# Three edits to the attention stage of a fused attention and two-MoE kernel: the decay array, one GpSimd wait, and when x is loaded

## The chip, the core and the metric

The program runs on one core of one Trainium2 chip. Its time is the device time in microseconds of one launch, from all inputs in HBM to the output in HBM. The program was run three times before the change; a profiled execution of its own gives the trace.

## What is computed

The reference does three things one after the other: causal attention with a decay per token (4 batches of 8 heads, 576 tokens, head width 64), a gated feed-forward block on the result, and a second MoE block with eight experts that each take a fixed number of tokens.

```python
# attention: one of 32 heads (4 batches x 8 heads), S = 576, D = 64
scores = scale * np.matmul(q, k.transpose(0, 1, 3, 2))
cum = np.cumsum(np.log(np.clip(f, 0.0001, 1.0)), axis=-1)
scores = np.where(causal, -1e9, scores + cum[..., :, None] - cum[..., None, :])
attn = softmax(scores)                     # with the row maximum taken off
x = (attn @ v)                             # to 2304 tokens x 512
x = (sigmoid(x @ w_gate) * (x @ w_val)) @ w_out        # 512 -> 1536 -> 512
# second block: each token goes to one of 8 experts, 288 tokens each
out[mask_e] = np.maximum(x[mask_e] @ w1[e], 0) @ w2[e]
```

All matrix products are made in float32 precision from two rounded parts (`fp32r`): a high part that ScalarE rounds, and a low part that GpSimd gets by a subtraction.

## The kernel before

**Stages.** Attention takes the first 201 us. `network` (L1183) builds the stages in that order; instructions go to each engine in the order in which the code is written, so what stands where in the loop decides what waits behind what.

**Attention, one head.** `prep(h)` (L131, L132, L135) has ScalarE round the raw q and k of a head into the tile `P` (five of them rotate). `decay(h)` (L139) and `copies(h)` (L143, L145) are DMAs from SBUF to SBUF: the decay rows into `P`, and q and k into the tile `p`. `query_low(h)` (L148) and `key_low(h)` (L152) are GpSimd subtractions that put the low parts into `p`. `maxparts(h)` multiplies q and k for the row maxima, which VectorE reduces (L177, tiles `mj` and `mx`); for head 0 alone the decay is added by a second set of products of `pick` and `ck`, while later heads have it in `P`. `rows(h)` turns the maxima over with one product (`pb<-identr,mx`), ScalarE copies them out (L215, tile `mr`), and a DMA stores them as row 66 of `P` (L218, `P<-mr`). `scores(h)` multiplies (`py`, `p1b`), ScalarE takes the exponent (L240, tile `e`), GpSimd masks the diagonal blocks (L244), and `av(h)` multiplies with v (`pv<-e,vf`).

**Order of the loop.** In round h the code writes `scores(h)`, then `av(h-1)`. Inside the products of `av` stand `early()`, which has `rows(h+2)`, `prep(h+4)`, `decay(h+5)` and `fill(h, 1)`, and `late()`, which has the maxima of head h+3. Then come `copies(h+3)`, the store of finished outputs or loads of q, k and v, `query_low(h+4)`, `key_low(h+2)`, and last `fill(h, 0)`. So a head's maxima are stored in round h-2 and read at the start of round h. SyncE (SP) issues all these DMAs in that same order, one after the other.

**The decay.** `ft` takes the 32 rows of f twice, on 64 partitions (L74): the source is an access pattern with a first dimension of two and a stride of zero. VectorE clips it (L119), ScalarE takes the logarithm (L120), VectorE sums it up (L122) and writes the rounded decay `ck` (L123) and, on the lower 32 rows, what the rounding lost (L124). Nine products without a use (`warm`, `py<-identb`) run on TensorE meanwhile, and more stand between the first maxima.

**What `fill` does.** Between heads it prepares the next stage: it cuts weights of the gated block into high and low parts (45 steps on VectorE at L437, L440 and L443 for 15 pieces, each followed by L451 on ScalarE and L454 on GpSimd; the list `BITS` says how many steps come after which head), and it loads the x of batch 0. That x comes in four pieces of two heads: `X.load` (L484, L485) issues four DMAs of 128 KB for each (two of the attention output `xs` into `xal`, two of the reciprocal row sums `rec`, broadcast to 64 partitions); `X.split` multiplies them on VectorE (L498), rounds on ScalarE (L500) and subtracts on GpSimd (L502). Before, the four loads stand at the ends of rounds 23, 24, 25 and 26, and the multiplications in rounds 27 to 30.

Of the kernel before, what the change touches and what calls it, by code (L numbers as in the profile page):

```python
# [6 lines left out]
F32 = mybir.dt.float32  # L7
# [10 lines left out]
B, H, S, D = 4, 8, 576, 64  # L18
NHEAD = B * H
# [41 lines left out]
def attention(ev, qk, vr, f, xs, rec, fill, W):  # L61
# [3 lines left out]
    nc, tc = ev.nc, ev.tc  # L65
    with ExitStack() as ctx:
# [4 lines left out]

        W.third = st
        ft = st.tile([128, S], F32, name="ft")[:2 * NHEAD]
        nc.sync.dma_start(ft, bass.AP(tensor=f.tensor, offset=f.offset, ap=[[0, 2], [S, NHEAD], [1, S]]))  # L74

        RAW, VF = {}, {}
        RAW4 = [st.tile([128, 2, S], F32, name=f"raw{i}") for i in range(4)]
# [20 lines left out]
        idle = st.tile([2 * NHEAD, 1], F32, name="warm")  # L98
# [18 lines left out]
        ck = st.tile([2 * NHEAD, S], F32R, name="ck")  # L117
# [11 lines left out]
        def prep(h, key=False):  # L129
            p1, r = P1[h % 5], RAW[h]  # L130
            nc.scalar.activation(p1[0:64, Q0:K0], r[0:64], AF.Copy)  # L131
            nc.scalar.activation(p1[0:64, K0:], r[64:128], AF.Copy)  # L132
            P2[h] = wk.tile([128, 2 * S], F32R, name="p2", bufs=4)
            if key:
                nc.scalar.activation(P2[h][64:128, S:], r[64:128], AF.Copy)  # L135
# [5 lines left out]
        def copies(h, keys=True):  # L141
            p1, p2 = P1[h % 5], P2[h]
            nc.sync.dma_start(p2[0:64, :S].bitcast(F32), p1[0:64, Q0:K0].bitcast(F32))  # L143
            if keys:
                nc.sync.dma_start(p2[64:128, S:].bitcast(F32), p1[0:64, K0:].bitcast(F32))  # L145

        def query_low(h):
            nc.gpsimd.tensor_tensor(P2[h][64:128, :S], RAW[h][0:64], P1[h % 5][0:64, Q0:K0], op=OP.subtract)  # L148
# [147 lines left out]
        warm(WARM[0])  # L296
        prep(0, True)
        copies(0, False)
        query_low(0)
        prep(1, True)  # L300
        key_low(0)
# [86 lines left out]
TC = 512  # L388
# [786 lines left out]

EARLY = 15
KO = (0, 1, 3, 4, 2)
XL = 23
FIRST = {3: (0, 1), 6: (2,)}
BITS = [0] * 5 + [(3 * i + 1) // 2 for i in range(23)] + [34, 35, 38, 41, 45]  # L1180
PRE = 0


def network(tc, qk, vv, f, ww, bcT, w1, w2, cb, cf, out):
    nc = tc.nc
    ev = Env()
    ev.nc, ev.tc = nc, tc
    with ExitStack() as ctx:
        ctx.enter_context(tc.manual_schedule())

        def pool(name, stack=ctx, side="left", bufs=1, **kw):
            return stack.enter_context(tc.tile_pool(name=name, bufs=bufs, side=side, reuse_waits="tile", **kw))

        ev.consts = pool("consts")
        dr = ctx.enter_context(tc.tile_pool(name="dram", bufs=1, space=bass.MemoryType.DRAM))
        xs = dr.tile([NHEAD, D + 1, S], F32, name="xs")
        rec = dr.tile([NHEAD, S], F32, name="rec")
        x2d = dr.tile([N, DM], F32, name="x2d")
        L = ev.consts.tile([128, E, NT], F32, name="L")
        ev.idx = ev.consts.tile([TT, 24], I32, name="idx")  # L1200
        ev.consts.tile([128, 48], F32, name="space")

        body, right = ExitStack(), ExitStack()
        xp = pool("xp", right, "right")
        w0, mix = pool("w0", body), pool("mix", body)
        W = Weights(ev, mix, ww)
        W.tiles(w0, 0, -(-EARLY // 3))
        X = XLoader(ev, xp, xs, rec)
        xa = X.tiles(xp, "xa")
        X.put(0, xa)  # L1210
        X.put(2, xa)
        X.put(4, xa)

        xr = [None]

        def fill(h, lag):
            if lag == 0 and h in FIRST:
                for n in FIRST[h]:
                    W.load(n)
            if lag == 0:  # L1220
                if 0 <= h - XL - 4 < 4:
                    X.split(0, h - XL - 4, steps=(0,))
                for i in range(BITS[h], BITS[h + 1]):
                    W.bits(*divmod(i, 3))
                if 0 <= h - XL < 4:
                    if (h - XL) % 2 == 0:
                        xr[0] = W.third.tile([128, 2, S], F32, name=f"raw{(h - XL) // 2}")
                    X.load(0, h - XL, r=xr[0][:, (h - XL) % 2, :TC])
            else:
                if 0 <= h - XL - 5 < 4:  # L1230
                    X.split(0, h - XL - 5, steps=(1, 2))
                for lag, step in ((1, 0), (2, 1)):
                    if lag <= h < NHEAD + lag:
                        for i in range(BITS[h - lag], BITS[h - lag + 1]):
                            n, s = divmod(i, 3)
                            if s == 2:
                                W.cut(n, (step,))

        attention(ev, qk, vv, f, xs, rec, fill, W)
        W.third = None  # L1240

        W.tiles(pool("w1", body), -(-EARLY // 3), NF)
        work, ps = ExitStack(), ExitStack()
        xq = pool("xq", right, "right")
        W.more, W.ahead = xq, 4
        xb = X.tiles(xq, "xb")
        X.put(1, xb)
        X.put(3, xb)
        F = Ffn(ev, W, X, EARLY, bcT, x2d, L, pool("pg", ps, bufs=4, space=PSUM), pool("po", ps, space=PSUM))
        F.wk, F.mix, F.right = pool("fw", work), mix, xq  # L1250
        F.wp = F.wk.tile([128, 128], F32, name="wp")[:, :NF * E].rearrange("p (f e) -> p f e", e=E)
        F.regular()
        rest, left = F.defer(lambda: xd), 7 * 3 * NF

        def filler(n):
            nonlocal left
            for _ in range(min(n, left)):
                next(rest, 0)
                left -= 1

        F.group(filler)
        right.close()
        work.close()

        ep = pool("ep", side="right")
        tail = ExitStack()
        rp, rw = pool("rp", tail), pool("rw", tail, bufs=2)
        scratch = [mix.tile([128, n], F32, name=m, bufs=1) for m, n in (("mr0", 1024), ("mr1", 1024), ("mb0", 512), ("mb1", 512))]
        xd, scratch[0] = scratch[0][:, :DM], scratch[0][:, DM:]
        EW = Experts(ev, ep, w1, w2)  # L1270
        nc.vector.memset(xd, 0.0)
        F.store(LAST, xd)
        R = Route(ev, rp, rw, F.bank, cb, cf, scratch, filler)
        EW.load(0)
        F.logits(scratch[1], filler)
        R.start(L)
        for r in range(ROUNDS):
            R.round(r == 0, FILL[5] if r < ROUNDS - 1 else 6, lambda: r and EW.split((r - 1) // 2, (r - 1) % 2, R.c[:1, 0, :1, 0]))
        a = R.settle()
        R.permutation(a)  # L1280
        X0 = First(ev, ep, scratch, x2d)
        X0.tokens(R)
        for part in range(2):
            EW.split(3, part, X0.hot[:1, :1])
        filler(left - 2 * 3 * NF)
        X0.gather()
        filler(left)
        next(rest, 0)
        X0.turn(xd, F.bank)
        tail.close()  # L1290
        body.close()
        ps.close()
        EW.pool = pool("ew")
        xw = pool("xw", bufs=2)
        pools = {n: pool("xp_" + n, bufs=b, space=PSUM) for n, b in (("t", 3), ("y", 2), ("h", 3))}
        experts(ev, EW, x2d, X0.x, ev.idx, out, xw, lambda n: pools[n].tile([128, 512], F32, name="e" + n))


def layout(inputs):

    import numpy as np
    q, k, v = (np.asarray(inputs[n]).reshape(NHEAD, S, D) for n in "qkv")
    qk = np.concatenate([q.transpose(0, 2, 1), k.transpose(0, 2, 1)], 1).reshape(NPAIR, 2, 2 * D, S).transpose(0, 2, 1, 3)
    rows = np.r_[0:512, 448:576].reshape(5, 128)
    vv = v.reshape(NPAIR, 2, S, D)[:, :, rows].transpose(0, 3, 2, 1, 4)
    vv = np.concatenate([vv, np.ones(vv.shape[:-1] + (2,), vv.dtype)], -1)
    vv[:, :64, 4] = 0.0
    cols = [np.asarray(inputs[n]).reshape(4, 128, NF, 128).transpose(2, 1, 0, 3).reshape(NF, 128, 512)
            for n in ("moe_w_gate", "moe_w_val")]
    ww = np.concatenate(cols + [np.asarray(inputs["moe_w_out"]).reshape(NF, 128, DM)], 2)  # L1310
    cb, cf = route_constants()
    named = dict(qk=qk, vv=vv, f=np.asarray(inputs["f"]).reshape(NHEAD, S), ww=np.ascontiguousarray(ww).view(np.int64),
                 wg2=np.asarray(inputs["moe2_w_gate"]).T, w1=inputs["moe2_w1"], w2=inputs["moe2_w2"], cb=cb, cf=cf)
    return {n: np.ascontiguousarray(a) for n, a in named.items()}

# [12 lines left out]
```

## Time and profile before

| | |
|---|---|
| time, median of 3 runs | 906.77 us (906.17 to 911.58) |
| the profiled execution | 907.6 us, of which its span 905.9 us |
| TensorE busy | 879.4 us (97%) |
| VectorE, GpSimd, ScalarE busy | 59%, 50%, 38% |
| mean granted TensorE clock | 0.992 of full speed |
| moved by DMA | 110.99 MB, mean 123 GB/s |

TensorE is busy for 97% of the span, so its waits and its clock are read first. A busy TensorE is not one at its peak, since matmuls are pipelined and their ends modelled. Line numbers in the rows are those of the kernel before. `SPq` rows are DMA issues by SyncE: the time in them is that of the issue, not that of the transfer.

### The profile page before, as it was taken

To read this page: it belongs to the slowest core of one execution; us is meant where nothing else is said; L and a number is where in the kernel's file an instruction comes from. 1 tells how busy PE (TensorE), PEld (TensorE's weight loads), DVE (VectorE), ACT (ScalarE), POOL (GpSimd) and SP (SyncE) were. 2 spreads that over 40 slices of the span, in tenths; PEclk is the share of its full clock that TensorE was granted. 3 is DMA by queue.
4 is the path that set the end of the run, shared out by engine and by line. 5 is a ranking of instruction groups with operands and counts; after the bars stand their busy time and mean duration, and the time that the engine had idled before them with its cause. 6 is when DMAs were issued, how large, how long until landed. Compare 5 with 4: busy or idle time off the path is not lost. (4 is left out here: it accounts for less than half of the span.)

```text
span 905.9 us, 14131 instructions
## 1 busy us (share of the span) xinstructions
PE 879.4 (97%) x5193; PEld 748.7 (83%) x5193; DVE 535.7 (59%) x1182; ACT 343.8 (38%) x609; POOL 456.7 (50%) x387
## 2 busy tenths in 40 slices
PE   6999999889999999999999999999999999999995
PEld 3787788668788888888888887887799999999995
DVE  4457777558887398998989642435523443443431
ACT  4777777653333111121121222221036455444530
POOL 4678888764656113221232222231249878777741
PEclk9999999999999999999999999999999999999998
DMA  3687877755552202101021210011238766656610
GB/s 101 152 239 236 224 226 223 205 159 182 176 158 94 76 1 73 38 19 58 17 87 34 67 47 1 1 45 47 72 130 255 230 197 183 196 180 203 211 30 26
DMA packets 48983, 110.99 MB, mean 123 GB/s; under 512 B 11333, under 2 KB 11749, under 8 KB 48913
## 3 DMA queue, kind: packets, MB, share of 16 engines
q1 hardware_dynamic: 44753, 98.54, 36.7%
q0 software_dynamic: 3072, 9.44, 3.3%
q10 hardware_dynamic: 1088, 2.10, 0.7%
q8 instruction: 41, 0.67, 0.3%
q14 instruction: 29, 0.24, 0.1%
HBM read 86.06 MB, written 14.57 MB: 111 GB/s over the span
## 5 line engine op out<-in xcount | busy, mean ns | idle before, releaser
L542 POOL TENSOR_TENSOR gl<-sg,gh 128x512 fp32r<-128x512 f32 x36 | 49.7, 1382 | 186.4 <-ACT gh L541 186.4
L1026 POOL TENSOR_TENSOR elo<-eraw,ehi 128x1024 fp32r<-128x1024 f32 x46 | 110.4, 2411 | 33.8 <-ACT ehi L1024 33.4
L533 PE MATMUL gv<-xah,w_hi 128*128 128x512 f32 (+1 forms) x288 | 102.3, 355 | 0.0
L533 PE MATMUL gv<-xah,w_lo 128*128 128x512 f32 (+1 forms) x288 | 101.9, 354 | 0.0
L533 PE MATMUL gv<-xal,w_hi 128*128 128x512 f32 (+1 forms) x288 | 101.8, 354 | 0.0
L155 PE MATMUL pv<-e,vf 128*65 128x256 f32 (+1 forms) x434 | 96.6, 360 | 0.0
L575 DVE CUSTOM_DVE_ANT_0 mb<-mb,bc 128x512 f32<-128x512 f32 x96 | 82.2, 856 | 3.3
L575 DVE CUSTOM_DVE_ANT_0 mb<-mr,bc 128x512 f32<-128x512 f32 x96 | 80.6, 839 | 2.8
L541 ACT ACTIVATE gh<-sg 128x512 fp32r<-128x512 f32 x36 | 22.8, 633 | 151.6 <-DVE sg L538 73.2
L1118 PE MATMUL ey<-hh,ehi 128*128 128x288 f32 x256 | 77.7, 304 | 0.0
L1118 PE MATMUL ey<-hl,ehi 128*128 128x288 f32 x256 | 75.8, 296 | 0.4
L533 PE MATMUL gv<-xbh,w_hi 128*128 128x512 f32 x192 | 75.8, 395 | 0.0
L1118 PE MATMUL ey<-hh,elo 128*128 128x288 f32 x256 | 75.3, 294 | 0.0
L533 PE MATMUL gv<-xbl,w_hi 128*128 128x512 f32 x192 | 74.9, 390 | 0.0
L533 PE MATMUL gv<-xbh,w_lo 128*128 128x512 f32 x192 | 74.8, 390 | 0.0
L177 DVE CUSTOM_DVE_ANT_0 mj<-p1b,mq 128x192 bf16<-128x192 f32 (+1 forms) x116 | 42.3, 421 | 51.2 <-PE p1b L155 51.2
L155 PEld LDWEIGHTS pv<-e,vf 128*65 128x65 f32 x434 | 51.6, 139 | 21.3 <-issue 6.3
L1105 PE MATMUL eh<-xeh,ehi 128*128 128x288 f32 x224 | 67.6, 302 | 0.0
L1024 ACT ACTIVATE ehi<-eraw 128x1024 fp32r<-128x1024 f32 x60 | 63.3, 1055 | 9.7 <-DMA eraw<-w 9.6
L1105 PE MATMUL eh<-xeh,elo 128*128 128x288 f32 x224 | 65.9, 294 | 0.0
L1105 PE MATMUL eh<-xel,ehi 128*128 128x288 f32 x224 | 65.8, 294 | 0.0
L1108 DVE SCALAR_TENSOR_TENSOR hl<-eh,hh 128x288 fp32r<-128x288 f32 x64 | 29.0, 456 | 62.2 <-ACT hh L1107 56.5
(232 smaller groups left out, 2291.7 us busy)
## 6 DMA issues: line engine op xcount, KB each, us to landing
eraw<-w SPq DMA_DIRECT2D x56, 512.0 KB
mr<-ww SPq DMA_DIRECT2D x26, 512.0 KB
p<-P SPq DMA_DIRECT2D x62, 144.0 KB
raw<-qk SPq DMA_DIRECT2D x15, 576.0 KB
vf<-vv SPq DMA_DIRECT2D x16, 330.0 KB
bc<-ww SPq DMA_DIRECT2D x10, 512.0 KB
xs<-xo SPq DMA_DIRECT2D x16, 292.5 KB
x2d<-mr SPq DMA_DIRECT2D x17, 256.0 KB
```

Source lines behind the costliest of these rows:

```text
L155: nc.tensor.matmul(out, lhsT, rhs, start=start, stop=stop, skip_group_check=True)
L177: nc.vector.tensor_tensor_reduce(out=junk[:, JT[t]:JT[t] + n], in0=src, in1=ev.mq[:, S - n:], op0=OP.add, op1=OP.min, scale=-1.0, scalar=3 ...
L533: nc.tensor.matmul(p[i][:, :m], w_[:, ws], x_[:, k], start=n == 0, stop=n == 11)
L541: nc.scalar.activation(hi, s, AF.Copy)
L542: nc.gpsimd.tensor_tensor(lo, s, hi, op=OP.subtract)
L575: nc.vector.tensor_tensor_reduce(out=junk, in0=a, in1=self.bc[j], op0=OP.mult, op1=OP.add, scale=1.0, scalar=0.0, accum_out=res)
L1024: nc.scalar.activation(hi, r, AF.Copy)
L1026: eng.tensor_tensor(lo, r, hi, op=OP.subtract)
L1105: nc.tensor.matmul(p[:, :CH], w_[:, ws], x_[:, k], start=n == 0, stop=n == 11)
L1108: nc.vector.scalar_tensor_tensor(h[1][:, f], p[:, :CH], 0.0, h[0][:, f], op0=OP.max, op1=OP.subtract)
L1118: nc.tensor.matmul(p[:, :CH], w_[:, ws], h_[:, f], start=n == 0, stop=n == 23)
```

## The change

Three edits. The decay comes from the host as a plain array of 64 rows, the 32 rows of f twice, and `ft` is loaded from it as it stands. A copy of one element of `ck` is put on GpSimd ahead of its first subtraction, so that this waits until `ck` is written. The four loads of x stand in rounds 15, 19, 23 and 27, the multiplications two rounds after each, the rounding and the subtraction three rounds after; they use one tile `xr` of their own. The list `BITS` is written from a table of steps and has one step less in rounds 17, 21 and 25, and one more in each of rounds 30 and 31.

```diff
-        nc.sync.dma_start(ft, bass.AP(tensor=f.tensor, offset=f.offset, ap=[[0, 2], [S, NHEAD], [1, S]]))
+        nc.sync.dma_start(ft, f)
...
         copies(0, False)
+        nc.gpsimd.tensor_copy(idle[NHEAD:NHEAD + 1], ck[NHEAD:NHEAD + 1, :1].bitcast(F32))
         query_low(0)
...
-XL = 23
+XF = 15
 FIRST = {3: (0, 1), 6: (2,)}
-BITS = [0] * 5 + [(3 * i + 1) // 2 for i in range(23)] + [34, 35, 38, 41, 45]
+STEPS = {17: 1, 21: 1, 25: 1, 29: 3, 30: 4, 31: 5}
+BITS = [sum(STEPS.get(i, 1 + i % 2) for i in range(5, h)) for h in range(NHEAD + 1)]
...
             if lag == 0:
-                if 0 <= h - XL - 4 < 4:
-                    X.split(0, h - XL - 4, steps=(0,))
+                k, i = divmod(h - XF, 4)
+                if 0 <= k < 4 and i == 0:
+                    X.load(0, k)
+                if 0 <= k < 4 and i == 2:
+                    X.split(0, k, steps=(0,))
...
-                if 0 <= h - XL < 4:
-                    if (h - XL) % 2 == 0:
-                        xr[0] = W.third.tile([128, 2, S], F32, name=f"raw{(h - XL) // 2}")
-                    X.load(0, h - XL, r=xr[0][:, (h - XL) % 2, :TC])
             else:
-                if 0 <= h - XL - 5 < 4:
-                    X.split(0, h - XL - 5, steps=(1, 2))
+                k, i = divmod(h - XF, 4)
+                if 0 <= k < 4 and i == 3:
+                    X.split(0, k, steps=(1, 2))
...
-    named = dict(qk=qk, vv=vv, f=np.asarray(inputs["f"]).reshape(NHEAD, S), ...
+    named = dict(qk=qk, vv=vv, f=np.concatenate([np.asarray(inputs["f"]).reshape(NHEAD, S)] * 2), ...
```

On GpSimd, at the program's start, the rows of the change are these (`pick` is the helper matrix of head 0's decay, `warm` the tile with the one element, `p` the tile of low parts):

```order
L109 MEMSET pick 64x128
L111 MEMSET pick 1x128 x2
L299 COPY warm<-ck 1x1
L148 TENSOR_TENSOR p_156<-raw_103,P_107 64x576
L152 TENSOR_TENSOR p_156<-raw_103,p_156 64x576
L148 TENSOR_TENSOR p_163<-raw_103,P_107 64x576
```

Before, the row of L299 is not there and L148 follows the memsets. All the subtractions of GpSimd now stand behind that copy, and it waits for VectorE.

On SyncE, from the end of round 23 on, the kernel before issues this (`xal` and the broadcast into `raw` are the loads of x, `P<-mr` the store of a head's maxima):

```order
L484 DMA xal<-xs 64x512
L485 DMA raw_1773<-rec 64x512
L484 DMA xal<-xs 64x512
L485 DMA raw_1773<-rec 64x512
L218 DMA P_107<-mr 1x5x128
L139 DMA P_107<-ck 2x576
L143 DMA p_1736<-P_107 64x576
L145 DMA p_1736<-P_107 64x576
L83 DMA raw_106<-qk 128x1152
L484 DMA xal<-xs 64x512
L485 DMA raw_1773<-rec 64x512
L484 DMA xal<-xs 64x512
```

And the changed kernel on SyncE, from the end of round 15 on:

```order
L485 DMA xal<-xs 64x512
L486 DMA xr<-rec 64x512
L485 DMA xal<-xs 64x512
L486 DMA xr<-rec 64x512
L218 DMA P_107<-mr 1x5x128
L139 DMA P_107<-ck 2x576
L143 DMA p_1224<-P_107 64x576
L145 DMA p_1224<-P_107 64x576
L83 DMA raw_106<-qk 128x1152
L218 DMA P_107<-mr 1x5x128
L139 DMA P_107<-ck 2x576
L428 DMA mr_1359<-ww 128x512
```

Each load of x still stands ahead of the next head's `P<-mr`, but three rounds without one follow it, where before the next load followed after one head.

## Rows read from the trace of the kernel before

**Rows 1.** Waits of TensorE, 155 to 200 us: total, times, longest.

```profile
PE py L155 <- DMA P<-mr: 5.2, 3, 2.3
```

**Rows 2.** Timeline, 0 to 40 us: start, us, engine, line, operation, idle before it.

```profile
0.83 0.74 SPq L74 DMA_DIRECT2D ft<-f  x1
...
2.49 4.02 PE L155 MATMUL py<-identb 128*128 128x512 bf16 x9 [2.49 <-DVE identb L42]
...
8.59 0.45 DVE L119 TENSOR_SCALAR ft<-ft 64x576 f32<-64x576 f32 x1 [5.88 <-DMA ft<-f]
9.08 0.68 ACT L120 ACTIVATE ft<-ft 64x576 f32<-64x576 f32 x1 [6.04 <-DVE ft L119]
...
9.79 1.35 DVE L122 TENSOR_TENSOR_SCAN cum<-ft,zero 64x576 f32<-64x576 f32 x1 [0.75 <-ACT ft L120]
10.36 0.68 ACT L132 ACTIVATE P<-raw 64x576 fp32r<-64x576 f32 x1
...
10.42 1.94 POOL L148 TENSOR_TENSOR p<-raw,P 64x576 fp32r<-64x576 f32 x1 [7.30 <-ACT P L131]
...
11.09 1.27 PE L155 MATMUL p1b<-P 64*128 64x192 f32 x4 [4.58 <-ACT P L132]
11.18 1.49 DVE L123 TENSOR_SCALAR ck<-cum 64x576 fp32r<-64x576 f32 x1
...
12.70 1.84 DVE L124 SCALAR_TENSOR_TENSOR ck<-cum,ck 32x576 fp32r<-32x576 f32 x1
...
14.69 1.24 PE L155 MATMUL p1b<-ck,pick 64*128 64x192 f32 x4 [1.68 <-DVE ck L124]
...
20.48 0.67 PE L155 MATMUL pb<-identr,mx 128*5 128x128 f32 x1
...
21.88 1.26 PE L155 MATMUL py<-identb 128*128 128x512 bf16 x5
...
23.46 0.37 PE L155 MATMUL py<-P 67*128 67x256 f32 x1
...
27.16 0.35 PE L155 MATMUL py<-P 67*128 67x256 f32 x1 [0.92 <-DMA P<-mr]
```

**Rows 3.** Windows: busy time of PE, PEld, DVE, ACT, POOL; clock; DMA share; GB/s.

```profile
2.00:2.50 0.50, 0.01 (x1) 0.02 (x2) 0.50 (x4) 0.49 (x4) 0.45 (x2) 1.00 0.10 9
...
11.50:12.00 0.50, 0.50 (x3) 0.50 (x3) 0.50 (x1) 0.47 (x2) 0.50 (x1) 1.00 0.91 217
```

**Rows 4.** The same view, 28 to 31.5 us and 188.5 to 192 us.

```profile
28.00:31.50 3.50, 3.50 (x14) 2.82 (x13) 0.77 (x2) 1.95 (x5) 3.42 (x3) 0.51 0.97 251
188.50:192.00 3.50, 3.50 (x13) 2.80 (x12) 2.74 (x3) 1.67 (x4) 3.35 (x4) 0.51 0.95 270
```

**Rows 5.** Timeline, 150 to 170 us: ScalarE's copy of maxima, their store.

```profile
153.82 0.27 ACT L215 ACTIVATE mr<-pb 5x128 f32<-5x128 f32 x1
...
158.14 0.78 SPq L218 DMA_DIRECT2D P<-mr  x1
...
164.54 0.27 ACT L215 ACTIVATE mr<-pb 5x128 f32<-5x128 f32 x1
```

**Rows 6.** Timeline, 170 to 200 us, engines mixed.

```profile
172.72 0.78 SPq L218 DMA_DIRECT2D P<-mr  x1
...
174.81 0.59 SPq L145 DMA_DIRECT2D p<-P  x1
...
175.46 0.38 PE L155 MATMUL py<-P 67*128 67x256 f32 x1 [2.25 <-DMA P<-mr]
...
177.38 1.41 POOL L152 TENSOR_TENSOR p<-raw,p 64x576 fp32r<-64x576 f32 x1 [2.17 <-DMA p<-P]
...
182.81 0.68 DVE L440 SCALAR_TENSOR_TENSOR ft<-mr,ft 128x512 uint32<-128x512 uint32 x1
...
187.95 0.36 PE L155 MATMUL py<-P 67*128 67x256 f32 x1 [2.35 <-DMA P<-mr]
```

**Rows 7.** Windows of 10 us, columns as in rows 3, rounds before the loads.

```profile
140.00:150.00 10.00, 10.00 (x63) 8.05 (x62) 6.88 (x20) 7.74 (x15) 8.70 (x9) 1.00 0.83 239
```

More of the change, by code (lines that the diff above doesn't have):

```diff
@@ L1212, in network @@
         X.put(4, xa)
-        xr = [None]
         def fill(h, lag):
@@ L1311, in layout @@
     cb, cf = route_constants()
-    named = dict(qk=qk, vv=vv, f=np.asarray(inputs["f"]).reshape(NHEAD, S), ww=np.ascontiguousarray(ww).view(np.int64),
+    named = dict(qk=qk, vv=vv, f=np.concatenate([np.asarray(inputs["f"]).reshape(NHEAD, S)] * 2), ww=np.ascontiguousarray(ww).view(np.int64),
                  wg2=np.asarray(inputs["moe2_w_gate"]).T, w1=inputs["moe2_w1"], w2=inputs["moe2_w2"], cb=cb, cf=cf)
```

## The prediction

> **What bounds the kernel now.** I read the windows of 10 us first: TensorE is busy all through nearly every one, but at the program's start and near the end of attention. So it is the bound, and the change can give only what TensorE loses in two places, the program's start and the last heads of attention. The waits of TensorE name the second: 5.2 us in three waits for the store of a head's maxima, `P<-mr` [rows 1]. In the one row of rounds before the loads TensorE is busy 10.00 of 10.00 while the DMA engines are taken for 0.83 of their time [rows 7]. The timeline of the start gives the first place: TensorE's useful work begins at 11.09, it stops for 1.68 us ahead of head 0's decay products at 14.69, and head 0's scores begin at 23.46 [rows 2]. Last I read the clock. In two stretches of 3.5 us it is granted at 0.51, the lower of its two levels, 1.2 instead of 2.4 GHz [rows 4]; each follows a wait (0.92 us until 27.16, 2.35 us until 187.95) [rows 2, 6] and costs 3.5 x 0.49 = 1.7 us. At the start the column shows 1.00, but nine warm products take 4.02 us, 0.45 each, and five at 21.88 take 1.26, 0.25 each [rows 2]: the array works at its lower level until about 21 us.
>
> **The plain decay array.** The DMA of `ft` is issued at 0.83 and VectorE gets the data only at 8.59, 7.8 us later [rows 2]. From 2.0 to 2.5 us, before the loads of q and k move, the DMA share is 0.10, that is 1.6 of 16 engines [rows 3]. A transfer of exactly the new shape, 64 rows of 576 floats, is in the trace: `p<-P`. While the first of them moves, the share is 0.91 [rows 3], and one issued at 174.81 has let GpSimd go on at 177.38, 2.57 us later, in a busy queue [rows 6]. So `ft` should land at 0.83 + 2.6 = 3.4 us; I take 3.7, since the first transfer of the program began late (9 GB/s at 2.0 to 2.5). The bounds are 3.4 and, if nothing changes, 8.59. I lean to the near end because the shape is the same. The Trainium skill (DMA: Bandwidth & Descriptors, section on why a DMA increments its semaphore by 16) says that a copy runs on the largest number of engines up to 16 that divides the slowest dimension of both its sides; a source that begins with a dimension of two then gets two engines, a plain one of 64 rows gets sixteen. By it the landing would be some 0.3 us sooner than I take, and the sum below the same. The share of 0.10 agrees.
>
> What follows `ft` moves with it: clip 0.45, logarithm 0.68, sum 1.35 with some 0.1 us between them [rows 2], so the sum ends at about 6.3.
>
> **The GpSimd wait.** The two instructions that write `ck` take 1.49 and 1.84 us while the subtractions run [rows 2]. The clip, also a tensor-scalar on 64x576, takes 0.45 with GpSimd idle [rows 2]; a scalar-tensor-tensor of 512 takes 0.68 in a quiet place [rows 6], so 0.77 for 576. With GpSimd held, the pair should take 1.2 instead of 3.3: 2.1 us off, bounded by 0 (it is not GpSimd) and 2.1. `ck` is then ready at about 7.5 instead of 14.54. Behind the copy wait all subtractions; the first starts at 7.6 or so instead of 10.42, so even the waiting engine is ahead of its old times. If `ft` landed at 8.59 after all, it would start at 12.5, 2 us later than before, and head 0's scores need only the first two, done at some 15.5, far ahead of 23.46. The wait costs nothing.
>
> **What TensorE makes of it.** Head 0's products need the rounded keys (L132), which stand on ScalarE behind the logarithm [rows 2]. That ends near 4.9, two roundings of 0.7 follow, and the raw q and k, issued right behind `ft`, should be there by 5 (no row shows their landing; they were there by the rounding ahead of the one at 10.36). So the start is near 6.5, where the warm products end as well: 11.09 - 6.5 = 4.5 us. At 8.4 TensorE comes to the decay products and `ck` is there: the 1.68 us go too. Together 6.2 with everything behind at old speed. Between 14.69 and 20.48 TensorE has 5.8 us of work at the lower level. Before, it rose about 6.5 us after the gap that ended at 14.69; now there is no gap from 2.49 on, so I expect it high from some 9 us. At most 2.6 us of that stretch fall away, at least none; other steps (the reductions, the DMA of the decay rows) get in the way, and I take 1.5. **Start: -7.7**, between -6.2 and -9.0 if `ft` lands early, -1.7 if it doesn't.
>
> **The loads of x.** A load is four issues of about 0.6 us (`p<-P`, nearly the same shape, has 0.59 [rows 6]), 2.4 us on SyncE, and 512 KB, 2.1 us of the queue at 239 GB/s. Before, four such loads follow in four rounds, and SyncE falls behind: maxima ready at 153.82 + 0.27 are stored at 158.14, 4.0 us late, those of 164.54 at 172.72, 7.9 late [rows 5, 6]. The store is read two rounds on, and 2.7 us after the late issue at 172.72 TensorE starts, having stood 2.25 [rows 6]. Note that the first load alone, 4.0 us late, made no wait. Two rounds of regular work are 12 issues (the order on SyncE), about 7.2 us by the same 0.6, while two rounds take 10.7 (153.82 to 164.54 [rows 5]); so SyncE can make up 3.5 us in two rounds at most, and a load of 2.4 is made up before the next, four rounds later. On the queue, 0.83 is taken; 2.1 us more in four rounds of 5.4 make 0.93. The three waits go, 5.2 us, and with the last of them the stretch at half clock, 1.7: 6.9 at most. I take off a little for store and copies that come late around each load. **End: -6.5**, between -5.5 and -6.9.
>
> The moved steps themselves are the same in number. Four multiplications leave the last rounds of VectorE, and the three steps taken from rounds 17, 21 and 25 pay for the new ones; GpSimd gets a subtraction in rounds 18, 22, 26 and 30, hidden behind TensorE (8.70 of 10 busy [rows 7]; four of about 1.4 us in 80 us make it 9.4). The weights' last steps stand one round later at most, for a use in the next stage tens of microseconds on.
>
> **The sum.** The profiled execution took 907.6; 907.6 - 7.7 - 6.5 = 893.4. It lay 0.8 above the median of 906.8, so on the scale of medians 892.6.
>
> **Rivals.**
> 1. *`ft` lands no sooner* (it may queue with q and k whatever its form). For it: its 7.8 us cover the time in which those move too. Against: the share of 0.10 [rows 3]. Then the wait alone counts: `ck` at 12.4, TensorE ready at 13.0, 1.7 gained. 907.6 - 1.7 - 6.5 - 0.8 = 898.6. Chance 0.09.
> 2. *The waits move with the loads.* For it: the queue is taken for 0.83 before a byte is added, and 4.0 us of lateness came from one load. Against: that one made no wait. In the kernel before, a load cost 6.9 / 4 = 1.7; if it costs 0.7 to 1.7 in its new place, the end gains 4.1 to nothing: 895.0 to 899.1. Chance 0.15.
> 3. *The other side: each load in mid-attention makes two heads' stores late,* each with a wait as the long ones before and one stretch at the lower clock: 2.25 + 2.35 + 1.7 = 6.3 per load, 25.2 for four. 907.6 - 7.7 - 6.9 + 25.2 - 0.8 = 917.4. It decides from 14.6 / 4 = 3.7 us per load on. Against it is that the first load before made no wait, and that three rounds without a load follow each now. Chance 0.04.
>
> **How the numbers follow.** The forecast has 0.72, its own range 907.6 - 0.8 less 11.7 to 15.9: 890.9 to 895.1. A stretch at half clock after the wait at 27.16 may go as well, 1.7, which makes 889 the low end; the high end of 899 takes in rival 1 and nearly all of rival 2. About 1% (897.7 and 915.8) is what a measurement of this kernel can tell from no change. Faster by more: the forecast and two thirds of rival 2, 0.82. Within 1%: rival 1 and the rest of rival 2, 0.14. Slower: 0.04.
>
> **What the profile after would show.** `ft` clipped near 3.7; the two writers of `ck` at 0.45 and 0.8, `ck` ready near 7.5; no wait of TensorE ahead of `ck,pick`; head 0's scores near 15.8; no wait for `P<-mr` behind 155 us, and clock 1.00 in the last rounds; the gated block beginning some 14 us sooner. The prediction is wrong if the clip still starts past 8, if raw q and k hold ScalarE up past 6, if the level stays low up to head 0's scores (then 6.2 at the start), or if waits for `P<-mr` or `p<-P` stand in rounds 16, 20, 24 or 28.

## The result, and the profile after

The changed kernel takes **898.08 us** (median; 896.32 to 899.73), the kernel before, measured again beside it, 906.76. The ratio is 0.9892, with a 95% interval of 0.9852 to 0.9933. Two later measurements of the same kernel gave 0.9894 (0.987 to 0.9919) and 0.9911 (0.9885 to 0.9938). So the change is worth about 1%: faster beyond doubt, and just at the bound of what I had called faster by over 1% (897.7; the three medians are 898.08, 896.74 and 898.01). The time lies inside my range (889 to 899), but above the forecast's own range (890.9 to 895.1): the gain is 8.7 us between the medians and 11.3 between the two profiled executions (907.6 and 896.3), where 14.2 were forecast.

All numbers of the profile below come from that execution of 896.3 us, with a span of 894.3. Its timeline of the start (start, duration, engine, line, operation, idle before it):

```profile
0.82 0.60 SPq L74 DMA_DIRECT2D ft<-f  x1
...
3.03 0.96 SPq L104 DMA_DIRECT2D P<-P  x1
...
3.54 0.45 DVE L119 TENSOR_SCALAR ft<-ft 64x576 f32<-64x576 f32 x1 [0.82 <-DMA ft<-f]
...
6.13 0.45 DVE L123 TENSOR_SCALAR ck<-cum 64x576 fp32r<-64x576 f32 x1
...
6.44 0.82 PE L155 MATMUL p1b<-P 64*128 64x192 f32 x4
6.62 0.75 DVE L124 SCALAR_TENSOR_TENSOR ck<-cum,ck 32x576 fp32r<-32x576 f32 x1
...
7.51 0.72 PE L155 MATMUL p1b<-ck,pick 64*128 64x192 f32 x4
7.52 0.18 POOL L299 COPY warm<-ck 1x1 f32<-1x1 f32 x1 [4.40 <-ACT P L131]
7.79 1.42 POOL L148 TENSOR_TENSOR p<-raw,P 64x576 fp32r<-64x576 f32 x1
...
8.51 1.04 PE L155 MATMUL py<-identb 128*128 128x512 bf16 x4
...
10.21 1.12 SPq L139 DMA_DIRECT2D P<-ck  x2
...
12.03 0.72 PE L155 MATMUL pv<-P 66*128 66x192 f32 x4 [2.49 <-DMA P<-ck]
...
15.06 2.13 PE L155 MATMUL py<-identb 128*128 128x512 bf16 x5
...
17.54 0.36 PE L155 MATMUL py<-P 67*128 67x256 f32 x1
```

Beside [rows 2]: the decay is clipped at 3.54 instead of 8.59; the writers of `ck` take 0.45 and 0.75 instead of 1.49 and 1.84; the first useful products start at 6.44 instead of 11.09, and those of the decay follow at 7.51 without a wait. Then there is a **new wait**: 2.49 us for `P<-ck`, the DMA that puts the decay rows into head 0's operand (line 139). Before, TensorE never waited for it. Head 0's scores start at 17.54, 5.9 us sooner than the 23.46 of [rows 2].

The waits of TensorE, first from 0 to 40 us, then from 100 to 200 (total, times, longest):

```profile
PE pv L155 <- DMA P<-ck: 2.5, 1, 2.5
PE py L155 <- DVE identb L42: 2.5, 1, 2.5
PE py L155 <- DMA P<-mr: 1.2, 2, 0.9
...
PE py L155 <- POOL p L152: 0.7, 2, 0.4
PE pv L155 <- ACT xo L268: 0.5, 2, 0.3
```

The three long waits for `P<-mr` of [rows 1] are gone. Short ones for GpSimd's lower parts and for ScalarE's copy of the attention output stand there now. Windows of the same execution (length, busy PE, PEld, DVE, ACT, POOL, granted clock, DMA share, GB/s):

```profile
13.00:16.50 3.50, 3.50 (x12) 1.70 (x11) 2.03 (x10) 2.60 (x5) 2.01 (x2) 0.56 0.18 39
...
22.00:25.50 3.50, 3.50 (x24) 2.81 (x24) 1.10 (x5) 2.63 (x7) 3.43 (x3) 1.00 0.97 262
...
177.50:181.00 3.50, 3.50 (x22) 2.75 (x21) 3.43 (x5) 2.75 (x6) 2.00 (x2) 1.00 0.84 235
```

The two stretches at the lower clock of [rows 4] began behind the starts of head 1's and head 30's scores (27.16 and 187.95). These heads now start at 21.22 and 177.21, and the windows behind them are at 1.00. Up to the gated block the column falls in one place only: a new stretch stands behind the new wait, from 13.4 to 16.8. The warm products show it without the clock column: four take 1.04 us (0.26 each) ahead of the wait, and at 15.06 five take 2.13 (0.43 each).

Where the time went, from the starts of the heads' first score products and of the gated block in the two traces:

| Place | before | after | sooner by | forecast |
|---|---|---|---|---|
| head 0's scores | 23.46 | 17.54 | 5.9 | 7.7 |
| head 3's scores | 39.51 | 32.64 | 6.9 | 7.7 |
| head 20's scores | 129.47 | 122.61 | 6.9 | 7.7 |
| gated block | 200.87 | 188.50 | 12.4 | 14.2 |
| end of the span | 905.9 | 894.3 | 11.6 | 14.2 |

The gated block's first product, in the kernel after:

```profile
188.50 0.63 PE L534 MATMUL gv<-xah,w_hi 128*128 128x512 f32 x1
```

### The profile page after: what moved, and what is told of

It reads as the page before. It is cut to its first block, busy times and chain, and to the rows that moved or that the text cites. A ratio compares the mean times of both kernels' runs of the same rounds, so it can differ in the third digit from the quotient of the medians.

```text
span 894.3 us, 14148 instructions
## 1 busy us (share of the span) xinstructions
PE 874.4 (98%) x5193; PEld 745.0 (83%) x5193; DVE 536.0 (60%) x1182; ACT 342.8 (38%) x609; POOL 457.5 (51%) x388
```

## The experiments

Every ratio is against runs of the kernel before on the same chip. Their medians lay between 906.1 and 909.4, so ratios are compared, or the positions in the traces, and not times measured apart.

### The same kernel again

No edit; it goes along to measure the spread.

> The changed kernel as it is, again. In the first comparison its four runs spread from 896.3 to 899.7 us, 3.4 us, and the profiled one was the fastest. Theory A (the gain is what the profile shows: gated block begins 12.4 us sooner, 11.6 us of the span): median near 896, ratio 0.987 to 0.989. Rival B (the profiled run was lucky; an execution usually loses 2 to 3 us more, by the clock falling at another place): median near 898.5, and a second profile shows a further stretch at the lower clock or a wait that the first doesn't have.

Measured 896.74 us (895.61 to 899.88), ratio 0.9894. At the start it has the same picture: TensorE waits 2.2 us for `P<-ck`, head 0's scores begin at 17.52, and the lower clock stands from 13.6 to 17.0. In mid-attention the long rounds are not the same: 23 to 24 takes 6.75 us here and 5.78 in the first trace. So a single round's length is uncertain by about a microsecond. The median is nearer to theory A's 896 than to rival B's 898.5, and the trace has no further stretch at the lower clock, but its longest wait in mid-attention is 1.28 us where the first trace has 0.31. Ratios of 0.9892, 0.9894 and 0.9911 don't tell the two apart.

### Each part alone

The plain array alone, on the kernel before:

```
-        nc.sync.dma_start(ft, bass.AP(tensor=f.tensor, offset=f.offset, ap=[[0, 2], [S, NHEAD], [1, S]]))
+        nc.sync.dma_start(ft, f)
...
-    named = dict(qk=qk, vv=vv, f=np.asarray(inputs["f"]).reshape(NHEAD, S), ww=np.ascontiguousarray(ww).view(np.int64),
+    named = dict(qk=qk, vv=vv, f=np.concatenate([np.asarray(inputs["f"]).reshape(NHEAD, S)] * 2), ww=np.ascontiguousarray(ww).view(np.int64),
```

> The kernel before with the plain decay array alone. Theory A (the early landing makes the start): head 0's products at 6.5, ck slowed by GpSimd's subtractions to about 9.5 instead of 7.4, head 0's scores about 5 to 6 us sooner than 23.46, heads in mid-attention 5.5 to 6.9 us sooner; time 900 to 901.5. Rival B (the GpSimd wait is the larger half of the start): under 3 us gained, 904 or more.

The wait of GpSimd alone:

```
         copies(0, False)
+        nc.gpsimd.tensor_copy(idle[NHEAD:NHEAD + 1], ck[NHEAD:NHEAD + 1, :1].bitcast(F32))
```

> The kernel before with GpSimd's copy of one ck element alone. Theory A: the two writers of ck take 0.45 and 0.75 instead of 1.49 and 1.84, TensorE's 1.68 us ahead of the decay products goes, and 1 to 2.5 us come off: 904.3 to 905.8. Rival B (GpSimd's subtractions, 2 us later, hold up head 0's scores, or a clock stretch moves): 906.8 or slower.

The loads of x alone (the change's last two hunks of the kernel: `XF`, `STEPS`, `BITS` and `fill`):

```
-                if 0 <= h - XL - 4 < 4:
-                    X.split(0, h - XL - 4, steps=(0,))
+                k, i = divmod(h - XF, 4)
+                if 0 <= k < 4 and i == 0:
+                    X.load(0, k)
```

> The kernel before with the moved loads of x and the new table of steps alone. Theory A (places add up): no wait for P<-mr behind 155 us, the gated block begins 5.5 us sooner than 200.87; time 901 to 902. Rival B (the loads only moved their cost: new short waits of TensorE for GpSimd's low parts at rounds 21, 24 and 26 eat it): 903.5 or more.

| Part | median, us | ratio (95%) | head 0 | head 20 | gated block |
|---|---|---|---|---|---|
| plain array | 902.92 | 0.9944 (0.9924 to 0.9963) | -5.5 | -3.9 | -4.6 |
| GpSimd's wait | 905.21 | 0.9976 (0.9956 to 0.9997) | -1.6 | -1.6 | -2.5 |
| loads of x | 903.77 | 0.9955 (0.9937 to 0.9974) | 0.0 | +1.6 | -3.9 |
| sum of the three | | -1.25% | -7.1 | -3.9 | -11.0 |
| all three (after) | 898.08 | 0.9892 (0.9852 to 0.9933) | -5.9 | -6.9 | -12.4 |

(The last three columns are positions in the traces, less those of the kernel before.) Each part gains by itself, and in the measured times the three add up within the intervals. Only the wait of GpSimd came in at its forecast time. The plain array gives head 0 what was expected, but 902.92 us instead of 900 to 901.5; the loads of x take 903.77 instead of 901 to 902, a time that rival B had named. In both traces the way from head 0 to head 3 takes 1.6 us longer than before (17.69 and 17.65 instead of 16.05), with a stretch at the lower clock twice as long (21.7 to 28.5 and 27.7 to 34.5, before 28.1 to 31.5), though neither edit changes what is done there. The full change has no such stretch there. That is why the positions at head 20 don't add up. The timeline of the plain array alone:

```profile
3.64 0.45 DVE L119 TENSOR_SCALAR ft<-ft 64x576 f32<-64x576 f32 x1 [0.92 <-DMA ft<-f]
...
6.23 1.48 DVE L123 TENSOR_SCALAR ck<-cum 64x576 fp32r<-64x576 f32 x1
...
7.74 1.84 DVE L124 SCALAR_TENSOR_TENSOR ck<-cum,ck 32x576 fp32r<-32x576 f32 x1
...
9.73 1.24 PE L155 MATMUL p1b<-ck,pick 64*128 64x192 f32 x4 [1.37 <-DVE ck L124]
```

and of GpSimd's wait alone:

```profile
8.71 0.45 DVE L119 TENSOR_SCALAR ft<-ft 64x576 f32<-64x576 f32 x1 [5.99 <-DMA ft<-f]
...
11.29 0.45 DVE L123 TENSOR_SCALAR ck<-cum 64x576 fp32r<-64x576 f32 x1
11.78 0.75 DVE L124 SCALAR_TENSOR_TENSOR ck<-cum,ck 32x576 fp32r<-32x576 f32 x1
```

The two causes are cleanly apart. The form of the array alone moves the landing (3.64 against 8.71). The waiting GpSimd alone makes the writers of `ck` short (1.20 against 3.32 us). In both of these kernels, where the loads of x stand as before, TensorE still waits for a head's maxima near the end, once and longer (behind 100 us, the plain array alone):

```profile
PE py L155 <- DMA P<-mr: 3.5, 1, 3.5
```

The wait of GpSimd alone has 3.7 there. With the loads of x alone no wait for `P<-mr` is left behind 100 us, and from head 20 to the gated block the kernel gains 5.5 us, exactly what the full change gains there (12.37 - 6.86). So the gain at the end belongs to the loads, whatever the start does. Its +1.6 at head 20 is no cost of the loads, which begin only in round 15: it stands at head 3 already (41.15 against 39.51), behind that longer stretch. And rival B's short waits for GpSimd's low parts are there (0.7 us in two, behind 100 us), but they are in the 5.5 already.

### Without GpSimd's wait

The full change less the copy on GpSimd:

```
-        nc.gpsimd.tensor_copy(idle[NHEAD:NHEAD + 1], ck[NHEAD:NHEAD + 1, :1].bitcast(F32))
```

> The changed kernel without GpSimd's wait for ck. Theory A (since the decay rows wait for the ones until 10.2, what the wait saves at ck is hidden): ck is ready near 9.5 instead of 7.4, TensorE stands about 1.4 ahead of the decay products instead of 2.5 later on, head 0's scores lie within 0.5 us of 17.5, and the time is within 1 us of the changed kernel's. Rival B (the wait adds its own 1.7 to 2.2 us, as it does alone): head 0's scores near 19.5, 2 us slower.

Measured 899.02 us, ratio 0.9886 (0.987 to 0.9902). The writers of `ck` take 1.48 and 1.84 again, TensorE waits 1.96 us for them, and then not for `P<-ck`:

```profile
9.60 0.83 PE L155 MATMUL p1b<-ck,pick 64*128 64x192 f32 x4 [1.96 <-DVE ck L124]
...
10.32 1.11 SPq L139 DMA_DIRECT2D P<-ck  x2
```

Head 0's scores begin at 18.48, 0.9 us later than in the full change, and the time can't be told from it. The decay rows leave at 10.32 here and at 10.21 there, though `ck` is ready 2 us sooner there. So in the full change most of what the faster writers gain is lost again in the wait for `P<-ck`. What holds that DMA at 10.2 is the next question.

### What holds the decay rows

SyncE's own waits, which I had not read, name it. They are its waits from 0 to 40 us, first in the kernel before, then after:

```profile
SPq L139 <- DVE ck L124: 2.3, 1, 2.3
SPq L139 <- DMA P<-P: 1.3, 1, 1.3
```

```profile
SPq L139 <- DMA P<-P: 4.3, 1, 4.3
```

`P<-P` is the DMA of line 104 that fills the rows of ones (64 to 66) of the other four operands; 57 KB, issued at 3.03. The decay rows go into some of these rows, so line 139 waits for it. By SyncE's wait it lands at 10.2, behind the loads of q and k. Before, `ck` was ready at 14.54 and the fill had landed at about 12.2 (SyncE was free at 10.92 and waited 1.3): it was covered. Two experiments try it. First the same DMA is issued from ScalarE instead of SyncE:

```
-        nc.sync.dma_start(P1S[64:67, 1:].bitcast(F32), bass.AP(tensor=P1S.tensor, offset=P1S[64:65].offset, ap=[
+        nc.scalar.dma_start(P1S[64:67, 1:].bitcast(F32), bass.AP(tensor=P1S.tensor, offset=P1S[64:65].offset, ap=[
```

> The changed kernel, with the DMA that fills the rows of ones in P (P<-P) issued by ScalarE instead of SyncE, so that it doesn't stand behind the loads of q and k. In the changed kernel ck is ready at 7.37, but the decay rows of P are issued only at 10.21, and TensorE waits 2.5 us for them; SyncE's wait there names P<-P. Theory A (the fill of ones, late behind q and k, is what holds the decay rows): they are issued near 7.5, TensorE's wait for P<-ck goes from 2.5 to under 0.5, head 0's scores stand near 15 to 15.8 instead of 17.5, and 1.5 to 2.5 us come off. Rival B (SyncE or the queue is late whatever fills the ones): the decay rows are still issued past 9.5 and nothing is gained.

Measured 899.53 us, ratio 0.9874 (0.9854 to 0.9894): not to be told from the change. ScalarE issues the fill at 2.38, but the decay rows leave at 10.21 again:

```profile
SPq L139 <- DMA P<-P: 3.8, 1, 3.8
```

So the queue that issues it isn't what makes it late. TensorE stayed at its lower level until about 18 us in this trace, which left only 0.2 us of the wait, and head 0 began at 18.84. Then the DMA is taken out, and GpSimd sets the ones:

```
-        nc.sync.dma_start(P1S[64:67, 1:].bitcast(F32), bass.AP(tensor=P1S.tensor, offset=P1S[64:65].offset, ap=[
-            [P1S.ap[0][0], 3], [0, 4], [1, w]]).bitcast(F32))
...
+        for t in P1[1:]:
+            nc.gpsimd.memset(t[64:67].bitcast(F32), 1.0)
```

> The changed kernel without the DMA that fills the ones of P (P<-P); GpSimd sets them with four more memsets of 1.1 us each, in the time in which it waits for ck anyway. Issued by ScalarE instead of SyncE that DMA still landed so late that the decay rows were issued at 10.21. Theory A (it is the landing of that DMA alone, late by itself, that holds the decay rows): with it gone they are issued between 7.4 and 8.7, TensorE's wait for P<-ck (2.2 to 2.5 us) shrinks under 0.7, and head 0's scores stand 1.5 to 2.5 us sooner than 17.5, at 15 to 16, if the clock rises at the same place. Rival B (the memsets hold VectorE's clip and its writers of ck through GpSimd's and VectorE's common way into memory): clip and ck up to 1.1 us later each, and the gain is under 1 us.

Measured 897.78 us, ratio 0.9901 (0.9876 to 0.9925), beside 898.01 for the changed kernel measured with it: no difference. Its timeline:

```profile
3.17 4.57 POOL L111 MEMSET P<- 3x1216 f32 x4
...
3.58 1.01 DVE L119 TENSOR_SCALAR ft<-ft 64x576 f32<-64x576 f32 x1 [0.87 <-DMA ft<-f]
...
6.73 1.32 DVE L123 TENSOR_SCALAR ck<-cum 64x576 fp32r<-64x576 f32 x1
...
8.93 1.18 SPq L139 DMA_DIRECT2D P<-ck  x2
...
8.98 1.04 PE L155 MATMUL p1b<-ck,pick 64*128 64x192 f32 x4 [1.24 <-DVE ck L124]
...
11.92 1.47 PE L155 MATMUL pv<-P 66*128 66x192 f32 x4
```

The decay rows now leave 1.3 us sooner, as soon as `ck` is there (8.84), and TensorE doesn't wait for them: the fill was the cause. Nothing is gained. While GpSimd writes the ones, VectorE's clip takes 1.01 instead of 0.45 and the first writer of `ck` 1.32, so TensorE waits 1.24 for `ck`. It works at its lower level from 9.2 to 16.0, and head 0's scores begin at 17.88, where theory A had 15 to 16. So what the wait for `P<-ck` costs by itself isn't shown: taken away like this, it makes room for rival B's wait and an earlier stretch at the lower clock.

### The rounds with a load of x

In the full change four rounds behind head 20 are longer than the regular 5.28 us: 20 to 21 (5.95), 23 to 24 (5.78), 25 to 26 (5.82), 27 to 28 (5.69); 2.1 us together. (By the table `STEPS` round 27, too, has one weight step more than before, two instead of one, besides 30 and 31; but 27 to 28 takes 5.28 in both later traces of the change, so neither that step nor the load makes it long each time.) The first of them in the profile of after:

```profile
117.55 1.29 POOL L503 TENSOR_TENSOR xal<-xr,xah 128x512 fp32r<-128x512 f32 x1 [1.09 <-DMA p<-P]
...
118.80 1.72 POOL L455 TENSOR_TENSOR w_lo<-ft,w_hi 128x512 fp32r<-128x512 f32 x1
...
123.53 0.38 PE L155 MATMUL py<-p 128*128 128x256 f32 x1 [0.40 <-POOL p L152]
```

GpSimd subtracts for x and for a weight in one round, and the lower part of a key is late. In the first experiment x's subtraction goes to VectorE:

```
-                nc.gpsimd.tensor_tensor(xl, x, xh, op=OP.subtract)
+                (nc.vector if self.W.third else nc.gpsimd).tensor_tensor(xl, x, xh, op=OP.subtract)
```

> The changed kernel, with x's subtraction (L503) on VectorE instead of GpSimd during attention. In the changed kernel the rounds from head 20 to 21, 23 to 24 and 25 to 26 take 5.95, 5.78 and 5.82 us instead of 5.28, 1.7 us in all (2.4 in its second profile). Theory A (GpSimd falls behind in the rounds with an extra subtraction and hands over low parts late): at least the first of them is back at 5.3, and up to 1.7 us come off. Rival B (the transfers of q and k behind a load of x are late, which holds ScalarE's roundings): the rounds from 23 to 24 and 25 to 26 stay long, only 0.7 or nothing comes off.

Measured 903.47 us, ratio 0.9939 (0.9919 to 0.9959): slower than the change. Round 20 to 21 is back at 5.29, but 19 to 20 takes 6.28, 23 to 24 9.39 and 27 to 28 7.44. TensorE's waits show why:

```profile
PE p1b L155 <- DVE mx L177: 4.7, 3, 2.1
```

VectorE works in order, and head maxima now stand behind a subtraction that waits for its operands. A part of the loss isn't the edit's: in this trace the lower clock stands from 8.9 to 19.1 and head 0's scores begin at 19.65, while the edit acts from round 18 on. In the second, ScalarE's rounding and GpSimd's subtraction for the first load move from round 18 to 19:

```
-                if 0 <= k < 4 and i == 3:
-                    X.split(0, k, steps=(1, 2))
+                if h in (19, 22, 26, 30):
+                    X.split(0, (h - 18) // 4, steps=(1, 2))
```

> The changed kernel with the rounding and subtraction of the first piece of x one round later, in round 19 instead of 18, so that GpSimd has no round with both a weight's and x's subtraction before round 30. Theory A (the long round from head 20 to 21 is GpSimd falling behind in round 18): that round goes from 5.95 to 5.3 and 0.65 us come off; the round from 23 to 24 stays long. Rival B (the late transfers do it): the round stays at 5.9.

Measured 898.58 us, ratio 0.991 (0.9885 to 0.9935). Round 20 to 21 takes 5.29 instead of 5.94. ScalarE's rounding moved along, but the wait above names GpSimd, and with x's subtraction alone taken off GpSimd the round was regular too. So the double load on GpSimd did cost this round its 0.65 us, an amount too small for the whole time to show it.

In the third, each load of x is spread over two rounds:

```
-                if 0 <= k < 4 and i == 0:
-                    X.load(0, k)
+                if 0 <= k < 4 and i < 2:
+                    X.load(0, k, js=(i,))
```

(`load` then issues only the half `j in js` into the kept tile.)

> The changed kernel, with each load of x split into two halves of two DMAs, issued in two rounds one after the other (rounds 15 and 16, 19 and 20, and so on). Theory A (four issues and 512 KB at once put SyncE and the queue behind by some 2.5 us, and the next load of q and k comes too late for ScalarE): ScalarE's waits for raw<-qk in rounds 23 to 26 shrink from 1 to 2 us to under 0.5, the rounds from 23 to 24 and 25 to 26 go back to 5.3, about 1 us comes off. Rival B (GpSimd is the cause): the long rounds stay.

Measured 897.21 us, ratio 0.9872 (0.9852 to 0.9891). The later long rounds go by this row of the change measured again: ScalarE has to wait for the next raw q and k, rounds x and a weight behind it, and copies the attention output late.

```profile
138.71 0.69 ACT L131 ACTIVATE P<-raw 64x576 fp32r<-64x576 f32 x1 [1.93 <-DMA raw<-qk]
...
140.13 0.63 ACT L501 ACTIVATE xah<-xr 128x512 fp32r<-128x512 f32 x1
...
140.67 0.61 ACT L452 ACTIVATE w_hi<-mb 128x512 fp32r<-128x512 f32 x1
141.19 0.63 ACT L268 ACTIVATE xo<-pv 65x576 f32<-65x576 f32 x1
...
141.96 1.16 PE L155 MATMUL pv<-e,vf 128*65 128x256 f32 x4 [1.28 <-ACT xo L268]
```

With halves the wait for raw q and k doesn't stand there, and round 25 to 26 is back at 5.27. But 23 to 24 still takes 5.82, so that wait isn't its whole cause, and 27 to 28 takes 5.97: 1.9 us over the regular length in all, against 2.0 to 2.4 in the three traces of the change. The cost moves to another round more than it goes.

Last, the ones by memset, the later cut and the halves together, and the change a third time:

> The changed kernel with the ones by memset, the first piece of x cut a round later, and each load of x in two halves in consecutive rounds: all that the earlier runs point to. Theory A (the places are apart and add up): head 0's scores near 15.5, the rounds from 20 to 21 and from 23 to 27 within 0.3 us of 5.28, 3 to 4 us under the changed kernel. Rival B (what is taken off at the start comes back as a stretch at the lower clock, or the long rounds move elsewhere): within 1 us of the changed kernel.

> The changed kernel as it is, a third time, on the chip of the three runs above. Theory A (executions differ by where the clock falls at the start, not by the work): median 896 to 899, and at head 20 its scores differ from the other two profiles (122.61 and 122.09) by no more than one stretch of 3.5 us at the lower clock is worth, 1.7 us. Rival B: the rounds of mid-attention differ as well.

Measured 896.44 us, ratio 0.9884 (0.9859 to 0.9909), and 898.01, ratio 0.9911 (0.9885 to 0.9938). The intervals overlap, so none of these versions is known to beat the changed kernel. The three edits together are no sum of what each gave: head 0's scores begin at 17.86 and not near 15.5, with the lower clock from 9.2 to 16.1 and from 22.9 to 26.3, and rounds 23 to 24 and 27 to 28 take 6.26 and 5.98; that is what rival B said, though the medians lie 1.6 us apart and not within 1. The third trace of the change bears out both theories in part: at head 20 it stands at 123.10, within 1.0 us of the other two, but round 23 to 24 takes 6.31, and so differs in all three.

## Why the prediction was right, and where it fell short

**The array lands early: right.** Forecast 3.7 for the clip, measured 3.54. The DMA share from 2.0 to 2.5 us is now 0.59 instead of the 0.10 of [rows 3]:

```profile
2.00:2.50 0.50, 0.01 (x1) 0.01 (x1) 0.50 (x4) 0.49 (x4) 0.45 (x2) 1.00 0.59 129
```

The part alone shows that the form of the source does it. The rival in which `ft` lands no sooner is out.

**GpSimd's wait shortens the writers of `ck`: right.** Forecast 1.2 us for the pair, measured 1.20; `ck` is ready at 7.37, forecast 7.5, and the first subtraction starts at 7.79 instead of 10.42. The wait costs nothing, as forecast. Its worth was overstated in the full change: 2.1 us alone on the pair, but at most 0.9 at head 0's scores.

**TensorE's start: the times up to the decay products are right, the step behind them failed.** Forecast 6.5 for the first products and no wait ahead of `ck,pick`; measured 6.44 and none. For the stretch behind I had counted the DMA of the decay rows among "other steps" that "get in the way", and took 1.5 of 2.6 us as a gain. In the trace it is a wait of 2.49 us, because line 139 waits for the fill `P<-P`, which lands only 2.0 us sooner than before (10.2 instead of 12.2), while `ck` is ready 7.2 us sooner. The row that names this was in the trace of before (SyncE waited 1.3 us for it, hidden by `ck`). I asked what `ck` was late for, and not what else its store waited for. I expected the clock high from some 9 us: it was high from 6.44 to the new wait, and fell behind it; 3.5 us at 0.56 cost about 3.5 x 0.44 = 1.5 us. The sums: the decay products came at 7.51 and not 8.4, 7.2 us sooner than before where 6.2 were forecast; from there to head 0's scores it takes 10.03 us instead of 8.77, 1.3 longer where I had 1.5 less. Head 0's scores came at 17.54 instead of 15.8. The start's term was 7.7, measured 5.9. That the wait for `P<-ck` stands on this path is shown; that the 1.8 us come back without it is not (17.88 with the fill taken out).

**A gain that I had put into the low end came true.** From head 0 to head 3 the kernel takes 15.10 us instead of 16.05: the stretch at half clock behind the wait at 27.16 [rows 2, 4] is gone, although the wait itself remains (0.91 instead of 0.92). I had priced it at 1.7 and left it out of the sum; it gave 0.95. This was luck: the other two traces of the change gain 1.45 and 0.56 there, and that of the halved loads, whose start is the same code, gains nothing (16.04) and has the stretch. So at head 20 the start stands at 6.9 in this trace.

**The loads of x: right in mechanism, mis-sized by 1.0 us.** No wait for `P<-mr` stands behind 155 us, and the clock is 1.00 in the last rounds. Forecast -6.5, measured -5.5, my bound. I had counted the three waits and the clock as 6.9 and taken off 0.4 for what comes late around each load. Both were too small. Over rounds of regular length (5.28 us, and 4.45 and 4.39 for rounds 29 and 30, as the second trace of the change has them) the kernel before spends 7.9 us too much from round 20 to round 30, and the changed kernel 2.4. Of these, 2.1 are the four long rounds, and most of this is the second rival in small: a load in mid-attention costs about 0.5 us, short of the 0.7 from which that rival was counted. The measured time alone would fit that rival (895.0 to 899.1); the 5.5 us gained behind head 20 don't, since it had 4.1 at most. The first of these rounds is shown to come from GpSimd's second subtraction. I had called this subtraction hidden by its average (8.70 of 10 busy, 9.4 with the new work), and one round of the four was not. For the others the row of ScalarE's wait is what speaks, and the halved loads bear it out for round 25 to 26 only; it was not settled which part of the load delays the raw q and k. The third rival, slower than before, is out: no head's store is waited for.

**The rest of the gap.** The forecast sum was 14.2. Less 1.8 at head 0, plus 0.95 up to head 3, less 1.0 at the end, the gated block should begin 12.4 sooner, and does. Behind it the program takes 705.8 us instead of 705.0; in the traces of the other kernels this stretch has from 704.6 to 707.4, so I put the 0.8 down to spread. That leaves 11.6 of the span. The medians differ by less, 8.7, 10.7 and 8.1 us in the three measurements. The clock's stretches are part of this spread: the halved loads have the very same start as the change, and there TensorE is at the lower level from 8.7 to 15.6 and again from 22.4 to 25.8, while the change itself has it from 13.4 to 16.8 alone. That my range holds the time is partly luck, too: its high end, 899, was there for rivals 1 and 2, and what used it up was a start and an end that each gained less than forecast.

## What to carry to other kernels

When a result is made earlier, list every wait of the instruction that uses it, on the queue engines too: a transfer that was covered by the late result (here the fill of ones, 1.3 us of SyncE's wait before and 4.3 after) becomes the next bound. An average of 9.4 busy in 10 hides an engine only if its work is spread as evenly; two subtractions in one round cost 0.65 us. Several short terms of a start that each hold alone overlap when they are put together, so the last of them should be priced at what it still uncovers.

## What was unexpected of the hardware

- A fill of 57 KB between rows of one memory landed at 10.2, whether SyncE issued it at 3.03 us or ScalarE at 2.38, while the DMA of 64 plain rows had landed 2.7 us after its issue at 0.82. In the trace of the change its twelve packets of 4864 bytes move from 6.04 to 9.57, and from 3 to 8 us the DMA engines are taken for 0.85 or more of their time. Whether this load or the form of the fill makes it late wasn't settled.
- GpSimd slows VectorE not only with subtractions: beside memsets of three rows the clip of 64x576 took 1.01 us instead of 0.45, and the first writer of `ck` 1.32 instead of 0.45.
- The granted clock shows 1.00 at the program's start, while products of 512 columns take 0.43 us each, as they do in stretches where it shows about 0.5. In the run in which ScalarE issued the fill the column shows 1.00 all through attention, while products still take 0.43 us each at 16.37. Durations of like products tell the level there, the column doesn't.
- The place of the stretches at 1.2 GHz shifts from trace to trace: the same 0.9 us wait at the second head was followed by such a stretch in the kernel before and in the halved loads (0.92 us), and not in the changed kernel. The halved loads also have two short waits of TensorE at the start, 0.27 us until 6.26 and 0.37 until 7.73, and the lower level from 8.7; the change has neither wait, and the lower level from 13.4. That such small waits decide it was not tried.
